# Gaps between SBUF tiles, so that the right operand of every matrix product starts 64 bytes past its left operand modulo 256

## The chip, the core and the metric

One NeuronCore of a Trainium2 chip runs the whole kernel in one launch. The metric is device time in microseconds (us) for one execution. All other times below are from one profiled execution.

## The reference

An attention with a sigmoid in place of the softmax, followed by a channel mix with token shift. Everything is float32 (three weight matrices arrive as float64).

```python
scores = q @ k.T / sqrt(64) - log(448)          # batch 8, 12 heads, 448 tokens, head size 64
x = (sigmoid(scores) @ v) -> (8, 448, 768)
x_prev = x shifted by one token
xk = mu_k * x + (1 - mu_k) * x_prev
xr = mu_r * x + (1 - mu_r) * x_prev
r = sigmoid(xr @ w_r)                           # 768 x 768, the "receptance"
out = r * (maximum(xk @ w_k, 0)**2 @ w_v)       # 768 x 1024, then 1024 x 768
```

## The kernel before

An SBUF tile is a range of bytes that is the same in all 128 partitions. A matrix product on TensorE (PE) has a left operand, 64 or 128 columns that are loaded into the array (the profile's PEld rows), and a right operand, 448 columns that then stream through it (the PE rows). The load for the next product runs while the present one streams. A matrix with more digits than one pass keeps is split into a high part (fp32r) and the remainder, and a product is made of three: high by high, low by high, high by low.

The program has three parts, each with an order for every engine's queue that a planner (`Plan`) works out when the program is built.

- **Attention and receptance, interleaved.** For each of 48 pairs of heads, `scores` (L326) makes three chunks of 128 keys: three fp32r products for each of two heads, whose 64 rows sit in the two halves of the array, so that two matmuls run side by side. The left operands are `kh` and `kl`, the right ones `qh` and `ql`. The last 64 keys go through `score_tails` (L335; `kn` by `qn`, plain f32). ScalarE (ACT) makes the sigmoid from PSUM into `pf` and `pt`. `weigh` (L355) and `weigh_tails` (L364) multiply `vn` by `pf` and `pt` in plain f32, which takes two passes for each product. `gather` makes the shifted mix `xr`. From pair 8 on, `receptance` blocks are put between: 6 row tiles x 3 products = 18 matmuls (L396 to L398), left `wr_hi`/`wr_lo` in the tiles `slot0` to `slot2`, right `xr`. There are 48 blocks, 864 matmuls; the last eight run after the attention. VectorE (DVE) meanwhile converts the float64 weights.
- **First steps of the channel mix** (up to about 447 us) are made ready during those last eight blocks.
- **The channel mix.** `multiply` (L620) does both large products by a recursive scheme with seven block products instead of eight: 2 stages x 4 pairs of batches x 7 products, 36 matmuls each, 2016 in all. The left operands are in seven tiles: `slotb0` for the first product of a round, `slotc0` to `slotc2` for the next three, `slot0` to `slot2` for the last three. The right operands are a ring of twelve tiles `rr`, nine of them allocated in one place (`rr` in the profile) and three elsewhere (`rrb`); each has a high part and, 1792 bytes on, a low part. The results go to the PSUM banks `xb` and `yb`.

Where a tile lies follows from the order in which tiles are taken from their pools, left pools from low addresses up and right pools from high addresses down. Every offset that a product uses inside a tile (512, 1536, 1792, 2048, 3072, 3584 bytes and so on) is a multiple of 256, so a tile's start modulo 256 holds for all operands in it.

Of the kernel before, what the change touches and what calls it, by code (L numbers as in the profile page):

```python
# [8 lines left out]
F32 = mybir.dt.float32  # L9
F32R = mybir.dt.float32r  # L10
# [88 lines left out]
def attention_then_channel_mix(  # L99
# [15 lines left out]
    P = 128  # L115
    N, _, S = q.shape
# [36 lines left out]
    WP, PFB, PTB, LEAD, RAW = 512, 9, 2, 2, 4  # L153
# [5 lines left out]
    def ring(pool, name, bufs, shape, dtype):  # L159
        return [pool.tile(shape, dtype, name=f"{name}{i}") for i in range(bufs)]  # L160

    wp = ctx.enter_context(tc.tile_pool(name="wp", bufs=1, side="left"))
    rp, cv, att = ExitStack(), ExitStack(), ExitStack()
    rpool = rp.enter_context(tc.tile_pool(name="rpool", bufs=1, side="left"))
    cpool = cv.enter_context(tc.tile_pool(name="cpool", bufs=1, side="left"))
    ka = ctx.enter_context(tc.tile_pool(name="ka", bufs=1, side="right"))
    slots = ring(ka, "slotb", 1, [P, 2 * WO], F32R)
    wop = ring(ka, "wop", 1, [P, WO], F32)
    apool = att.enter_context(tc.tile_pool(name="apool", bufs=1, side="right"))
    ps, psc = ExitStack(), ExitStack()  # L170
    psum = ps.enter_context(tc.tile_pool(name="psum", bufs=1, space=PSUM))
# [2 lines left out]
    wr_slots = ring(wp, "slot", 3, [P, 2 * WO], F32R)  # L174
    wr_at = [wr_slots[t // 4][:, t % 4 * DM:(t % 4 + 1) * DM] for t in range(2 * NJ)]
    wr_hi, wr_lo = wr_at[0::2], wr_at[1::2]
    xr = ring(rpool, "xr", NJ, [P, 2, 2 * S], F32R)
    ro = ring(rpool, "ro", 2, [P, S], F32)
    wraw = ring(cpool, "wraw", 2, [P, WP, 2], U32)
    wbits = ring(cpool, "wbits", 8, [P, WP], U32)  # L180
    wexpo = ring(cpool, "wexpo", 1, [P, WP], U32)
    qn = ring(apool, "qn", RAW, [P, S], F32)
    kn = ring(apool, "kn", RAW, [P, S], F32)
    vn = ring(apool, "vn", 5, [P, NV, D], F32)
    qh = ring(apool, "qh", LEAD, [P, S], F32R)
    ql = ring(apool, "ql", LEAD, [P, S], F32R)
    kh = ring(apool, "kh", LEAD, [P, KW], F32R)
    kl = ring(apool, "kl", LEAD, [P, KW], F32R)
    pf = ring(apool, "pf", PFB, [P, 2, S], F32)
    pt = ring(apool, "pt", PTB, [P, 2, S], F32)  # L190
    xx = ring(apool, "xx", 2, [P, S + 1], F32)
# [309 lines left out]
    RB, YB = 9, 15  # L501
    kp = ctx.enter_context(tc.tile_pool(name="kp", bufs=1, side="right"))
    slots += ring(kp, "slotc", 3, [P, 2 * WO], F32R) + wr_slots
    wop += ring(kp, "wopb", 1, [P, WO], F32)
    x2 = ring(kp, "x2", 2, [P, S + 1], F32)
    ys = ring(kp, "ys", YB, [P, S], F32)
    rr = ring(kp, "rr", RB, [P, 2, S], F32R)
    for x in x2:
        nc.gpsimd.memset(x[:, 0:1], 0.0)

# [81 lines left out]
    xb = ring(pb, "xb", 4, [P, 512], F32)  # L592
    yb = ring(pb, "yb", 4, [P, 512], F32)
    vp = ctx.enter_context(tc.tile_pool(name="vp", bufs=1, side="left"))
    p1s = ring(vp, "p1s", 4, [P, S], F32)
    u2 = ring(vp, "u2", 4, [P, S], F32)
    cc = ring(vp, "cc", 5, [P, S], F32)
    rt_ = ring(vp, "rt", 3, [P, S], F32)
    ys += ring(vp, "ysb", 5, [P, S], F32)
    rr += ring(vp, "rrb", 3, [P, 2, S], F32R)  # L600
    nr[0] = nr[0] % len(rr)
    ncc, nrt = [0], [0]

# [125 lines left out]
```

## Time and profile before

| | us |
|---|---|
| median of 3 runs (861.77 to 862.41) | 862.13 |
| the profiled execution | 862.21 |
| its span, first to last instruction | 860.4 |
| PE busy | 843.5 |
| PE weight loads busy | 667.4 |
| DVE busy | 601.1 |
| ACT busy | 447.4 |

A matmul's duration in the profile reaches beyond the start of the next one, because matmuls are pipelined. So what a matmul costs is the time from its start to the start of the next; durations still tell groups apart.

### The profile page before, as it was taken

The page shows a single profiled execution, that of the slowest core. Times are in us where ns is not written, and L with a number is a line of the kernel's source. Part 1 is how long each engine was busy: PE and PEld are TensorE (multiplying, and loading weights), DVE is VectorE, ACT ScalarE, POOL GpSimd, SP SyncE. Part 2 cuts the span into 40 slices and gives each one's busy share as a digit, 9 for nine tenths or more (in the row PEclk, how much of TensorE's full clock was granted, in tenths as well). Part 3 has the DMA queues.
Part 4 walks back from the last instruction along what each step waited for, and adds up shares of the span by engine and source line. Part 5 has one row for each costly group of instructions (what it writes and reads, how often), then busy time and mean ns, then how long its engine had stood idle before and what let it go on. Part 6 is the DMA issues. An engine that isn't in the chain of part 4 may idle for free.

```text
span 860.4 us, 13233 instructions
## 1 busy us (share of the span) xinstructions
PE 843.5 (98%) x4704; PEld 667.4 (78%) x4704; DVE 601.1 (70%) x1115; ACT 447.4 (52%) x758; POOL 0.5 (0%) x8
## 2 busy tenths in 40 slices
PE   7999999999999999999999999999999999999998
PEld 3456666676666766667788999999999999999997
DVE  5999898988334323342479987969789795886955
ACT  7995555645546555464368384563746333233330
POOL 0000000000000000000000000000000000000000
PEclk9999999999999999999999999999999999999999
DMA  7878898888334433341487563343654667474415
GB/s 252 259 243 290 287 304 282 286 275 280 112 113 157 146 114 115 108 139 43 153 277 242 168 182 98 139 134 123 215 179 146 201 182 236 132 232 124 144 54 161
DMA packets 90930, 157.65 MB, mean 183 GB/s; under 512 B 10352, under 2 KB 79472, under 8 KB 90864
## 3 DMA queue, kind: packets, MB, share of 16 engines
q1 hardware_dynamic: 90864, 156.81, 55.8%
q8 instruction: 37, 0.61, 0.3%
q14 instruction: 29, 0.24, 0.1%
HBM read 98.05 MB, written 58.72 MB: 182 GB/s over the span
## 4 chain that ended last, share of the span: by engine, by line
PE 94%; ACT 3%; issue 1%; DMA 1%; DVE 1%; SPq 0%
PE xb L620 27%; PE yb L620 20%; PE av L355 12%; PE sc L326 10%; PE sc L396 7%; PE sc L398 7%; PE sc L397 7%; PE av L364 2%; PE sc L335 2%; ACT pf L347 1%; ACT t L379 1%; DMA qn<-in_q 1%; ACT qh L298 0%; ACT xx L374 0%; ACT pt L347 0%
## 5 line engine op out<-in xcount | busy, mean ns | idle before, releaser
L545 ACT CAST rr<-ys 128x448 fp32r<-128x448 f32 x135 | 73.7, 566 | 107.7 <-PE yb L620 41.7
L347 ACT ACTIVATE pf<-sc 128x896 f32<-128x896 f32 x144 | 125.4, 926 | 5.2 <-PE sc L326 5.2
L355 PE MATMUL av<-pf,vn 128*64 128x448 f32 x576 | 114.4, 544 | 0.0
L396 PE MATMUL sc<-xr,slot 128*128 128x448 f32 x288 | 107.8, 374 | 2.1 <-ACT pf L347 2.1
L398 PE MATMUL sc<-xr,slot 128*128 128x448 f32 x288 | 105.7, 367 | 0.0
L397 PE MATMUL sc<-xr,slot 128*128 128x448 f32 x288 | 105.6, 367 | 0.0
L620 PE MATMUL yb<-rr,slot 128*128 128x448 f32 x450 | 93.9, 364 | 0.0
L620 PE MATMUL xb<-rr,slotc 128*128 128x448 f32 x450 | 93.1, 362 | 0.8 <-ACT p1s L649 0.8
L546 DVE TENSOR_TENSOR rr<-ys,rr 128x448 fp32r<-128x448 f32 x135 | 80.4, 617 | 15.9 <-ACT rr L545 15.7
L299 DVE TENSOR_TENSOR kl<-kn,kh 128x384 fp32r<-128x384 f32 x48 | 26.7, 556 | 92.6 <-ACT kh L298 90.9
L620 PEld LDWEIGHTS xb<-rr,slotc 128*128 128x128 f32 x450 | 84.3, 188 | 6.9 <-ACT p1s L649 1.2
L620 PEld LDWEIGHTS yb<-rr,slot 128*128 128x128 f32 x450 | 84.4, 188 | 6.7
L355 PEld LDWEIGHTS av<-pf,vn 128*64 128x64 f32 x576 | 38.9, 136 | 62.5 <-issue 61.0
L402 ACT ACTIVATE ro<-sc 128x448 f32<-128x448 f32 x48 | 26.1, 544 | 79.3 <-PE sc L398 60.8
L326 PE MATMUL sc<-qh,kh 64*128 64x448 f32 x288 | 59.5, 409 | 7.4 <-ACT qh L298 4.4
L396 PEld LDWEIGHTS sc<-xr,slot 128*128 128x128 f32 x288 | 54.0, 188 | 13.7 <-ACT pf L347 8.4
L347 ACT ACTIVATE pt<-sc 128x896 f32<-128x896 f32 x24 | 22.2, 923 | 75.9 <-PE sc L335 75.9
L398 PEld LDWEIGHTS sc<-xr,slot 128*128 128x128 f32 x288 | 54.1, 188 | 5.0
L376 DVE COPY xx<-av 128x448 f32<-128x448 f32 x38 | 22.0, 621 | 51.4 <-PE av L364 51.4
L397 PEld LDWEIGHTS sc<-xr,slot 128*128 128x128 f32 x288 | 54.1, 188 | 4.7
L326 PEld LDWEIGHTS sc<-qh,kh 64*128 64x128 f32 x288 | 27.3, 186 | 37.7 <-issue 19.3
L326 PE MATMUL sc<-ql,kh 64*128 64x448 f32 x288 | 53.5, 368 | 0.0
(86 smaller groups left out, 1377.5 us busy)
## 6 DMA issues: line engine op xcount, KB each, us to landing
k_d<-cc SPq DMA_DIRECT2D x64, 224.0 KB, 2.0
kn<-in_k SPq DMA_DIRECT2D x48, 224.0 KB, 4.4
qn<-in_q SPq DMA_DIRECT2D x48, 224.0 KB, 4.7
vn<-in_v SPq DMA_DIRECT2D x48, 224.0 KB, 3.2
x_d<-xx SPq DMA_DIRECT2D x48, 224.0 KB, 3.8
r_d<-ro SPq DMA_DIRECT2D x48, 224.0 KB, 2.7
x<-x_d SPq DMA_DIRECT2D x48, 224.0 KB, 2.6
rt<-r_d SPq DMA_DIRECT2D x48, 224.0 KB, 2.9
```

The source lines that it names most:

```text
L299: op(DVE, dve(w), at, lambda src=src, hi=hi, lo=lo: nc.vector.tensor_sub(lo[i], src, hi[i]), R + [(a + "h", i)], [(a + "l", i)])
L326: nc.tensor.matmul(sc[u][:, h, :S], kk[half[h], c * P:(c + 1) * P], qq[half[h], :], start=e == 0, stop=e == 2)
L347: op(ACT, act(2 * S), at, lambda: nc.scalar.activation(f, sc[u][:, :, :S], AF.Sigmoid, bias=NEG_LOG_S, scale=SCALE), R, [K])
L355: nc.tensor.matmul(av[n % 2][half[h], :S], vn[n % 5][:, h * NC + c, :], pf[i][:, h, :], start=c == 0, stop=False)
L376: op(DVE, dve(S), at, lambda: nc.vector.tensor_copy(x[:, 1:], av[n % 2][:, :S]), [("av", n % 2)], [X])
L396: nc.tensor.matmul(t[:, :S], wr_hi[j][:, rows], hi, start=(j == 0), stop=False)
L397: nc.tensor.matmul(t[:, :S], wr_lo[j][:, rows], hi, start=False, stop=False)
L398: nc.tensor.matmul(t[:, :S], wr_hi[j][:, rows], lo, start=False, stop=(j == NJ - 1))
L402: op(ACT, act(S), at, lambda: nc.scalar.activation(ro[u], t[:, :S], AF.Sigmoid), [tk], [("ro", u)])
L545: op(ACT, act(S, True), at, lambda: nc.scalar.copy(r[:, 0], y), [Y], [R])
L546: op(DVE, dve(S), at, lambda: nc.vector.tensor_sub(r[:, 1], y, r[:, 0]), [Y, R], [R + ("lo",)])
L620: nc.tensor.matmul(bank[:, :S], a, b, start=first and t == 0 and e == 0, stop=t == n - 1 and e == 2, skip_group_check=True)
```

## The change

`gap` takes a tile that nobody uses, and by that shifts the tiles allocated after it. `qn`, `rr` and `ys` also change places with others. The built programs have the same instructions in the same order on every engine, with the same waits on the same semaphore values; the addresses alone differ. These are the starts modulo 256 in the two programs, and how far the right operand lies past the left one:

```
products           left tile  right tile   before: left right  past    after: left right past
scores             kh, kl     qh, ql              160   160      0            160   224   64
score tails        kn         qn                  160   160      0            160   224   64
weigh              vn         pf                  160   160      0            160   224   64
weigh tails        vn         pt                  160   160      0            160   224   64
receptance         slot       xr                   32    32      0             32    96   64
channel mix        slotc      rr                  160   224     64             32    96   64
channel mix        slotb      rrb                 224    32     64             32    96   64
channel mix        slotc      rrb                 160    32    128             32    96   64
channel mix        slot       rr                   32   224    192             32    96   64
channel mix        slotb      rr                  224   224      0             32    96   64
channel mix        slot       rrb                  32    32      0             32    96   64
```

```diff
+    def gap(pool, name, size):
+        pool.tile([P, size // 4], F32, name=name)
+
...
     wop = ring(ka, "wop", 1, [P, WO], F32)
+    gap(ka, "gap4", 192)
...
+    gap(rpool, "gap0", 64)
     xr = ring(rpool, "xr", NJ, [P, 2, 2 * S], F32R)
...
-    qn = ring(apool, "qn", RAW, [P, S], F32)
     kn = ring(apool, "kn", RAW, [P, S], F32)
     vn = ring(apool, "vn", 5, [P, NV, D], F32)
+    gap(apool, "gap1", 64)
+    qn = ring(apool, "qn", RAW, [P, S], F32)
     qh = ring(apool, "qh", LEAD, [P, S], F32R)
     ql = ring(apool, "ql", LEAD, [P, S], F32R)
+    gap(apool, "gap2", 192)
     kh = ring(apool, "kh", LEAD, [P, KW], F32R)
     kl = ring(apool, "kl", LEAD, [P, KW], F32R)
+    gap(apool, "gap3", 64)
     pf = ring(apool, "pf", PFB, [P, 2, S], F32)
...
     slots += ring(kp, "slotc", 3, [P, 2 * WO], F32R) + wr_slots
+    gap(kp, "gap5", 64)
+    rr = ring(kp, "rr", RB, [P, 2, S], F32R)
+    ys = ring(kp, "ys", YB, [P, S], F32)
     wop += ring(kp, "wopb", 1, [P, WO], F32)
     x2 = ring(kp, "x2", 2, [P, S + 1], F32)
-    ys = ring(kp, "ys", YB, [P, S], F32)
-    rr = ring(kp, "rr", RB, [P, 2, S], F32R)
+    gap(kp, "gap6", 128)
...
+    gap(vp, "gap7", 64)
+    rr += ring(vp, "rrb", 3, [P, 2, S], F32R)
     p1s = ring(vp, "p1s", 4, [P, S], F32)
...
     ys += ring(vp, "ysb", 5, [P, S], F32)
-    rr += ring(vp, "rrb", 3, [P, 2, S], F32R)
```

## Rows read from the trace of the kernel before

**Rows 1.** Windows: busy us of each engine by stage, granted clock, DMA share and rate.
```profile
core 0: us, PE busy (x) PEld busy (x) DVE busy (x) ACT busy (x) POOL busy (x), PEclk, DMA share, GB/s
0.00:80.00 80.00, 69.45 (x463) 37.41 (x464) 66.14 (x141) 66.48 (x112) 0.33 (x6) 1.00 0.78 252
...
120.00:140.00 20.00, 20.00 (x124) 14.04 (x123) 19.25 (x39) 10.36 (x16) 0.00 (x0) 1.00 0.94 317
...
215.00:430.00 215.00, 215.00 (x1312) 145.06 (x1309) 77.07 (x142) 109.01 (x171) 0.13 (x2) 1.00 0.36 120
...
456.00:857.00 401.00, 400.27 (x1980) 371.21 (x1980) 321.87 (x567) 180.54 (x332) 0.00 (x0) 1.00 0.52 164
```

**Rows 2.** Waits of PE from 80 us on: us in total, times, longest.
```profile
PE xb L620 <- issue: 1.4, 1, 1.4
PE xb L620 <- ACT p1s L649: 0.8, 1, 0.8
```

**Rows 3.** Instructions by line, PE, channel mix: busy us, mean ns, idle before.
```profile
L620 PE MATMUL xb<-rr,slotc 128*128 128x448 f32 x450 | 93.1, 362 | 0.8 <-ACT p1s L649 0.8
L620 PE MATMUL xb<-rrb,slotb 128*128 128x448 f32 x63 | 13.3, 363 | 0.0
L620 PE MATMUL yb<-rr,slot 128*128 128x448 f32 x450 | 93.9, 364 | 0.0
L620 PE MATMUL xb<-rr,slotb 128*128 128x448 f32 x225 | 47.1, 365 | 1.4 <-issue 1.4
L620 PE MATMUL xb<-rrb,slotc 128*128 128x448 f32 x126 | 26.9, 365 | 0.0
L620 PE MATMUL yb<-rrb,slot 128*128 128x448 f32 x126 | 27.3, 368 | 0.0
```

**Rows 4.** Chain that ended last, channel mix: start us, us, what.
```profile
463.31 7.20 PE yb L620 x36
470.51 7.34 PE xb L620 x36
...
485.13 7.28 PE xb L620 x36
...
528.52 7.43 PE yb L620 x36
```

**Rows 5.** Matmuls that read rrb or slotc: duration ns min/median/max, first and last start.
```profile
L620 PE MATMUL yb<-rr,slotc x198: 360/363/368, 463.2 to 824.9; 128*128 128x448 f32 x198
```

**Rows 6.** Receptance, by line: busy us, mean ns, idle before.
```profile
L396 PE MATMUL sc<-xr,slot 128*128 128x448 f32 x288 | 107.8, 374 | 2.1 <-ACT pf L347 2.1
L397 PE MATMUL sc<-xr,slot 128*128 128x448 f32 x288 | 105.6, 367 | 0.0
```

**Rows 7.** Timeline of PE inside one pair's scores, two matmuls side by side.
```profile
339.20 0.37 PE L326 MATMUL sc<-qh,kl 64*128 64x448 f32 x2
...
340.64 0.37 PE L326 MATMUL sc<-ql,kh 64*128 64x448 f32 x2
```

**Rows 8.** Attention's matmuls by line: duration ns min/median/max, first and last start.
```profile
L326 PE MATMUL sc<-qh,kh x288: 358/365/738, 4.4 to 402.7; 64*128 64x448 f32 x144
L355 PE MATMUL av<-pf,vn x576: 539/539/591, 13.3 to 415.2; 128*64 128x448 f32 x192
L335 PE MATMUL sc<-qn,kn x192: 536/536/587, 9.2 to 400.9; 64*64 64x448 f32 x192
L364 PE MATMUL av<-pt,vn x192: 536/562/587, 20.1 to 416.2; 64*64 64x448 f32 x192
```

**Rows 9.** Chain that ended last, end of receptance and first channel-mix product.
```profile
446.08 1.42 issue
447.49 3.90 PE xb L620 x18
```

**Rows 10.** DVE's remainders of rr and rrb from 456 us on: busy us, mean ns, idle.
```profile
L546 DVE TENSOR_TENSOR rr<-ys,rr 128x448 fp32r<-128x448 f32 x127 | 75.4, 617 | 15.7 <-ACT rr L545 15.7
...
L546 DVE TENSOR_TENSOR rrb<-ys,rrb 128x448 fp32r<-128x448 f32 x39 | 23.3, 618 | 2.4 <-ACT rrb L545 2.4
```

## The prediction

> **What bounds the kernel now.** I read the windows by stage first. Before 80 us PE is busy for 69.45 of 80 us and waits for the engines around it. [...] The list of PE's waits confirms it: after 80 us there are two, of 1.4 and 0.8 us [rows 2], both where receptance hands over to the channel mix. So a nanosecond that a matmul loses or gains after 80 us is a nanosecond of the kernel, as long as no other engine is about to become the bound. The one place where another nearly is, is around 130 us: DVE is busy for 19.25 of 20 us and the DMA engines for 0.94 of the time. In the channel mix DVE has 321.87 of 401 us, ACT half of that [rows 1].
>
> Then I ask whether a matmul's cost depends on where its operands lie. The channel mix answers that by itself, because one source line with one shape runs there on six pairings of tiles. The chain gives the cost of 36 matmuls, the rows by line give the mean duration of one for each pairing:
>
> - slotc by rr, 64 bytes past: 7.20 us for 36, that is 200.0 ns each; mean duration 362.
> - slot by rr, 192 past: 7.28 us, 202.2 ns; mean 364.
> - slotc by rrb, 128 past: 7.34 us, 203.9 ns; mean 365.
> - slot by rrb, 0 past: 7.43 us, 206.4 ns; mean 368 [rows 3, 4].
>
> Duration less 162 ns is the cost, to within 0.5 ns, in all four; so the two pairings that have no piece of their own in the chain can be read too: slotb by rr, 0 past, mean 365, 203 ns; slotb by rrb, 64 past, mean 363, 201 ns [rows 3]. The reader is to see that this is no property of a tile: slotc is the quick one with rr and not with rrb, slotb is the quick one with rrb and not with rr. What goes with the cost is the distance of the two operands. Both pairings at 64 are the cheapest, both at 0 are dearer.
>
> **The change, part by part.** No instruction, order or wait differs, so nothing is added or moved; the reserved bytes cost no time. The sum is over the products whose distance becomes 64, each priced by its present cost less the 200 ns (duration 362) of the pairing that has 64 now.
>
> *Channel mix, 2016 matmuls.* 711 are at 64 already (450 + 198 of slotc by rr, 63 of slotb by rrb): nothing. Slot by rr: 450 + 198 = 648 times (364 - 362) = 1.3 us. Slotb by rr: 225 x 3 = 0.7 us. Slotc by rrb: 126 + 90 = 216 x 3 = 0.65 us. Slot by rrb: 216 x 6 = 1.3 us. Together 3.9 us. (Of each pair of counts one row stands in the list; the other row, with x198 or x90, has the same mean within 1 ns.)
>
> *Receptance, 864 matmuls, all at 0.* The second and third lines have means of 367 (the first, 374, holds the stalls with which blocks begin) [rows 6]. If they come to 362: 864 x 5 = 4.3 us. This is not quite a copy of the channel mix: there the high and the low right operand alternate 1792 bytes apart, here three products in a row read addresses that agree modulo 512. That order at 64 is not in the trace. Bounds: nothing from below, and 367 - 360 = 7 ns from above, the shortest single duration that slotc by rr shows [rows 5], 6.0 us. I take 5 ns, because the two pairings at 64 agree within 1 ns although their high and low parts stand the other way round modulo 512.
>
> *Scores, 432 double matmuls, at 0.* Eight starts in a row span 1.44 us, 205.7 ns from one to the next [rows 7], and the median duration is 365 with a minimum of 358 [rows 8]. Two matmuls in the two halves of the array at distance 64 are in no row. Bounds: nothing, and the 7 ns to the minimum. I take 4 ns, toward the nearest rows (205.7 to about 201), and count 330 of the 432: those before 80 us are hidden in PE's waits, and one in nine ends in a change to another kind of product, whose pause the address has no part in. 1.3 us, at most 2.3.
>
> *Plain f32 products* (weigh and both kinds of tails), at 0. Weigh is 539 in the minimum and in the median, the key tails 536 in both [rows 8]: no scatter, while the scores, also at distance 0, have 358 and 365. I cost them at nothing. The cover for that is that an f32 pass streams more slowly: 448 columns in about 377 ns (539 less the same 162), nearly twice the 200 of an fp32r product, so a weight read has more room beside it. If that cover fails it is the slower rival below.
>
> *Other engines.* Addresses move for DVE, ACT and DMAs as well. DVE's remainders for rr (start 224 modulo 256) take 617 ns and for rrb (start 32) 618 [rows 10]: nothing.
>
> *What is not kept.* Two receptance blocks run before 80 us beside PE's waits (36 x 5 = 0.2 us). The last eight blocks (144 x 5 = 0.7 us) end in a wait of 1.42 us before the first channel-mix product [rows 9]; the chain names nothing that ended it ("issue"), but that product's operands come from loads through ACT and DVE, which an earlier PE would find no earlier. I lose half of the 0.7. Together 0.55 us.
>
> Sum: 3.9 + 4.3 + 1.3 - 0.55 = 9.0 us. The profiled execution took 862.21, 0.08 over the median of the runs, and 1.8 over its span; so 862.2 - 9.0 = 853.2 us.
>
> [...] The rows show 362 to 368 ns, 200.0 to 206.4 ns start to start, for the same product under different distances [rows 3, 4]. [...]
>
> **Rivals.**
>
> 1. *Only the channel mix gains* (5 in 100). Its distances are priced by rows of its own; receptance and scores might not be helped, if in their order of operands 64 is as bad as 0. Against it: slotb by rrb and slotc by rr are two orders, and both are quick. 862.2 - 3.9 = 858.3 us.
>
> 2. *Another engine becomes the bound between 80 and 215 us* (5 in 100). There DVE converts weights with the DMA engines at 0.94 near 130 us [rows 1], and about 135/366 of what runs between 80 and 446 us lies in that stretch, by time 305 of 828 receptance matmuls and 120 of 330 double ones: 305 x 5 + 120 x 4 = 2.0 us would turn into waits. Against: PE has no wait at all in it now, and its queue would come only 2% sooner to DVE's work. 853.2 + 2.0 = 855.2 us.
>
> [...]
>
> 4. *Slower: the f32 passes leave their flat level* (4 in 100). Weigh and tails make 288 + 48 + 48 = 384 passes (576 rows in pairs, 192 in fours). They were never seen at 64. If each went from 539 to the 591 that is their longest now [rows 8], 384 x 52 = 20 us, and the sum is 862.2 - 9.0 + 20 = 873 us. It decides from 9.0 / 384 = 23 ns a pass on, and makes the kernel slower by over 0.2% from 28 ns on. For it: an f32 pass loads 64 columns beside a stream of another pace, so its best distance need not be that of fp32r. Against: f32 at distance 0 shows no loss at all, and a slower stream has room.
>
> **The numbers.** The forecast has 80 in 100, with the time of its sum, 853.2 us. The range: with the upper bounds of receptance and scores 862.2 - 3.9 - 6.0 - 2.3 = 850.0; with the lower bounds 858.3, which takes in rivals 1 and 2. Outside are rivals 3 and 4 and a few in 100 of misjudged sizes. A measurement of this kernel tells 0.2%, 1.7 us, from no change. Faster by more: forecast and rivals 1 and 2, 90 in 100; within: 6; slower: 4.
>
> **What would show it.** In the profile after, all six pairings of L620 have a mean of 362 to 363, and every 36 matmuls in the chain take 7.20 to 7.25 us where no stall is; receptance's second and third lines have 362, the scores' median is near 360, weigh stays at 539. The first channel-mix product starts some 5 us earlier than at 447.49 us [rows 9], and the channel mix is about 4 us shorter. The prediction is wrong if receptance stays at 367, if weigh rises above 539, if PE's list of waits between 80 and 440 us is no longer empty, or if pairings at 64 still differ from each other.

## The result and the profile after

The changed kernel takes 852.93 us (median of 6 runs, 852.26 to 854.2), the kernel before 861.95 (6 runs, 859.24 to 863.33): a ratio of 0.9903, 95% interval 0.9887 to 0.9919, so 9.0 us faster. The two profiled executions differ by 862.21 - 852.26 = 9.95 us.

The matmuls of the changed kernel by line and shape (count, busy us, mean ns of one, idle before); line numbers have moved, L633 is `multiply`, L406 to L408 are receptance, L365 is weigh:

```profile
L365 PE MATMUL av<-pf,vn 128*64 128x448 f32 x576 | 114.4, 544 | 0.0
L406 PE MATMUL sc<-xr,slot 128*128 128x448 f32 x288 | 106.6, 370 | 2.1 <-ACT pf L357 2.1
L407 PE MATMUL sc<-xr,slot 128*128 128x448 f32 x288 | 104.3, 362 | 0.0
...
L633 PE MATMUL xb<-rr,slotc 128*128 128x448 f32 x450 | 93.0, 362 | 0.4 <-ACT p1s L662 0.4
L633 PE MATMUL yb<-rr,slot 128*128 128x448 f32 x450 | 92.9, 362 | 0.0
...
L633 PE MATMUL xb<-rr,slotb 128*128 128x448 f32 x225 | 46.5, 362 | 1.4 <-issue 1.4
...
L633 PE MATMUL xb<-rrb,slotc 128*128 128x448 f32 x126 | 26.5, 362 | 0.0
L633 PE MATMUL yb<-rrb,slot 128*128 128x448 f32 x126 | 26.5, 362 | 0.0
...
L633 PE MATMUL xb<-rrb,slotb 128*128 128x448 f32 x63 | 13.2, 362 | 0.0
```

The reader is to see that the six pairings, 362 to 368 before [rows 3], are one number now, and that receptance's second and third lines came down by 5 ns, from 367 to 362, its first one by 4 [rows 6]. The chain that ended last (start us, us, what) agrees: 7.20 us for every 36 matmuls, where there were 7.20, 7.28, 7.34 and 7.43 [rows 4].

```profile
457.49 7.20 PE yb L633 x36
464.69 7.20 PE xb L633 x36
471.89 7.20 PE yb L633 x36
479.09 7.20 PE xb L633 x36
```

PE's waits after 80 us (us in total, times, longest) have not grown; the second one has halved [rows 2]:

```profile
PE xb L633 <- issue: 1.4, 1, 1.4
PE xb L633 <- ACT p1s L662: 0.4, 1, 0.4
```

And by stage (busy us by engine, clock, DMA share and rate) PE is as full as before, beside a DVE that is no more of a bound than it was [rows 1]:

```profile
120.00:140.00 20.00, 20.00 (x126) 13.91 (x126) 18.63 (x37) 10.58 (x17) 0.00 (x0) 1.00 0.95 325
...
450.00:846.00 396.00, 395.98 (x1980) 371.09 (x1980) 320.97 (x565) 180.91 (x332) 0.00 (x0) 1.00 0.52 166
```

Where the time came from, by the starts of matmuls in the two traces: the first channel-mix product starts at 442.14 us instead of 447.49 (5.35 us), and from there to the start of the last matmul it is 403.79 us instead of 408.41 (4.62 us). Together 9.97, which is the whole difference of the two spans (860.4 and 850.5 us).

The attention's durations (ns min/median/max, first and last start): the scores came down by 2 ns in the first row's median and by 3 in the second, whose row before stands on top; weigh did not move [rows 8].

```profile
L326 PE MATMUL sc<-qh,kl x288: 355/362/572, 4.9 to 402.9; 64*128 64x448 f32 x144
...
L336 PE MATMUL sc<-qh,kh x288: 357/363/739, 4.5 to 397.9; 64*128 64x448 f32 x144
L336 PE MATMUL sc<-qh,kl x288: 357/359/572, 5.0 to 398.1; 64*128 64x448 f32 x144
...
L365 PE MATMUL av<-pf,vn x576: 539/539/590, 12.9 to 410.2; 128*64 128x448 f32 x192
```

### The profile page after: what moved, and what is told of

It is laid out like the page before. It is cut to its first block, busy times and chain, and to the rows that moved or that the text cites. A ratio compares the mean times of both kernels' runs of the same rounds, so it can differ in the third digit from the quotient of the medians.

```text
span 850.5 us, 13233 instructions
## 1 busy us (share of the span) xinstructions
PE 834.7 (98%) x4704; PEld 667.2 (78%) x4704; DVE 600.5 (71%) x1115; ACT 447.6 (53%) x758; POOL 0.5 (0%) x8
## 4 chain that ended last, share of the span: by engine, by line
PE 90%; ACT 4%; DMA 3%; issue 1%; DVE 1%; SPq 0%; POOLq 0%; POOL 0%; DVEq 0%; ACTq 0%
PE xb L633 26%; PE yb L633 20%; PE av L365 12%; PE sc L336 10%; PE sc L406 6%; PE sc L407 6%; PE sc L408 6%; DMA x<-x_d 2%; PE av L374 2%; PE sc L345 2%; ACT pf L357 1%; ACT t L389 1%; DMA qn<-in_q 1%; ACT qh L308 0%; ACT xx L384 0%
## 5 line engine op out<-in xcount | busy, mean ns | idle before, releaser
L365 PE MATMUL av<-pf,vn 128*64 128x448 f32 x576 | 114.4, 544 | 0.0
L406 PE MATMUL sc<-xr,slot 128*128 128x448 f32 x288 | 106.6, 370 | 2.1 <-ACT pf L357 2.1
L407 PE MATMUL sc<-xr,slot 128*128 128x448 f32 x288 | 104.3, 362 | 0.0
L408 PE MATMUL sc<-xr,slot 128*128 128x448 f32 x288 | 104.2, 362 | 0.0
L633 PE MATMUL xb<-rr,slotc 128*128 128x448 f32 x450 | 93.0, 362 | 0.4 <-ACT p1s L662 0.4
L633 PE MATMUL yb<-rr,slot 128*128 128x448 f32 x450 | 92.9, 362 | 0.0
L633 PEld LDWEIGHTS xb<-rr,slotc 128*128 128x128 f32 x450 | 84.3, 187 | 6.4 <-ACT p1s L662 0.8
L633 PEld LDWEIGHTS yb<-rr,slot 128*128 128x128 f32 x450 | 84.4, 187 | 5.6
L365 PEld LDWEIGHTS av<-pf,vn 128*64 128x64 f32 x576 | 38.9, 136 | 62.4 <-issue 61.3
L406 PEld LDWEIGHTS sc<-xr,slot 128*128 128x128 f32 x288 | 54.0, 188 | 12.6 <-ACT pf L357 8.3
L408 PEld LDWEIGHTS sc<-xr,slot 128*128 128x128 f32 x288 | 54.0, 187 | 3.7
```

The costliest lines, as they stand in the source:

```text
L365: nc.tensor.matmul(av[n % 2][half[h], :S], vn[n % 5][:, h * NC + c, :], pf[i][:, h, :], start=c == 0, stop=False)
L406: nc.tensor.matmul(t[:, :S], wr_hi[j][:, rows], hi, start=(j == 0), stop=False)
L407: nc.tensor.matmul(t[:, :S], wr_lo[j][:, rows], hi, start=False, stop=False)
L408: nc.tensor.matmul(t[:, :S], wr_hi[j][:, rows], lo, start=False, stop=(j == NJ - 1))
L633: nc.tensor.matmul(bank[:, :S], a, b, start=first and t == 0 and e == 0, stop=t == n - 1 and e == 2, skip_group_check=True)
```

## The experiments

The theory: what a fp32r matmul costs beyond the 200.0 ns of the cheapest pairing [rows 4] depends on the distance of its right operand to the left operands, modulo 256. Rivals: the new order of the tiles made the gain, or the place of one operand alone. In the `all_at` runs one number, DIST, replaces 64 in the changed kernel's gaps; the order of the tiles, the instructions and their order stand as in the changed kernel. `gap` now takes its size modulo 256, and `gap6` makes up for `gap5`. The attention's tiles as a whole lie 64 - DIST bytes further on modulo 256 than in the changed kernel.

```diff
-        pool.tile([P, size // 4], F32, name=name)
+        if size % 256:
+            pool.tile([P, size % 256 // 4], F32, name=name)
...
-    gap(rpool, "gap0", 64)
+    gap(rpool, "gap0", DIST)
...
-    gap(apool, "gap1", 64)
+    gap(apool, "gap1", DIST)
...
-    gap(apool, "gap2", 192)
+    gap(apool, "gap2", 256 - DIST)
...
-    gap(apool, "gap3", 64)
+    gap(apool, "gap3", DIST)
...
-    gap(kp, "gap5", 64)
+    gap(kp, "gap5", DIST)
...
-    gap(kp, "gap6", 128)
+    gap(kp, "gap6", 192 - DIST + 256)
...
-    gap(vp, "gap7", 64)
+    gap(vp, "gap7", DIST)
```

**All distances 0** (DIST = 0).

> The changed kernel with every right operand back at distance 0 modulo 256 from its left one, in the changed kernel's order of tiles (rr before ys, kn before qn and so on). Distance theory: the gain goes again. Channel mix: mean durations back to about 365 (as slotb by rr, whose parts stood in this order modulo 512, 203 ns each), receptance's second and third lines back to 367, scores' median to 364 or 365, weigh 539. 2016 x 2.8 + 864 x 5 + 330 x 4 = 11.3 us more than 852.9: about 864 us. Rival, the other order of the tiles made the gain (other neighbours for what DVE and ACT write): the time stays at 853, with 362 for the channel mix.

Measured: 861.23 us, median of 10 runs, ratio to the kernel before 1.0021 (0.9992 to 1.005), where about 864 was expected. Mean durations of 365 in the channel mix and in receptance:

```profile
L410 PE MATMUL sc<-xr,slot 128*128 128x448 f32 x288 | 105.2, 365 | 0.0
L636 PE MATMUL xb<-rr,slotc 128*128 128x448 f32 x450 | 94.2, 365 | 0.5 <-ACT p1s L665 0.5
```

So the gain hangs on the distance, not on the order of the tiles, which is the changed kernel's here. Two things were off. Receptance has the very addresses that it had before, and costs 365 instead of 367. And two of the ten runs took 867.99 and 870.84 us, the other eight 859.74 to 862.18.

**Both operands 64 bytes on** (distance 64 kept).

```diff
-    gap(ka, "gap4", 192)
+    gap(ka, "gap4", 384)
...
+    gap(wp, "gap8", 64)
     wr_slots = ring(wp, "slot", 3, [P, 2 * WO], F32R)
```

> Distance 64 kept, but both operands of every product 64 bytes further on: left at 96 and right at 160 modulo 256 in receptance and channel mix, left 224 and right 32 in the attention. Distance theory: nothing changes, 852.9 us, 362 for receptance and channel mix. Rival, the place of one operand alone counts (left at 32 or right at 96): the groups go back toward 364 to 368 and the time toward 858 to 864.

Measured: 853.65 us, median of 4 runs, ratio 0.9915 (0.99 to 0.993).

```profile
L408 PE MATMUL sc<-xr,slot 128*128 128x448 f32 x288 | 104.4, 363 | 0.0
...
L634 PE MATMUL yb<-rr,slot 128*128 128x448 f32 x450 | 92.9, 362 | 0.0
L634 PE MATMUL xb<-rr,slotc 128*128 128x448 f32 x450 | 92.9, 362 | 0.0
```

Both operands have moved by 64 bytes and the matmuls cost what they did, so the place of one operand alone does not explain the gain.

**The other distances.** DIST = 128, then 32, 96 and 192, then 160 and 224.

> Every distance 128. Distance theory: all pairings of the channel mix like slotc by rrb before, mean 365 with singles from 358 to 373; receptance and scores 2 to 4 ns dearer than at 64; 852.9 + 2016 x 3.5 + 864 x 3.5 + 330 x 3 = 864 us. Rival, only distance 0 is bad and all else is good: 853. Weigh 539 in both.

> Every distance 32. In the runs so far the start-to-start times within one run of like products settle into a repeating pattern: 200.0 ns on average at 64, 204.0 at 128, 202.2 at 192, and at 0 either 202.7 or 206.7. If the collision is between pieces of 64 bytes, 32 lies half in the piece of 0 and half in that of 64 and comes out between, 200 to 203: 853 to 860 us. If any gap that keeps the two streams apart will do, 200.0 and 853 us. Rival, 32 is worse than 0: over 861.

> Every distance 96, half way from 64 to 128. Pieces of 64 bytes: between 200.0 and 204.0 ns, 853 to 863 us. If 64 is only the edge of a good stretch: 200.0 or less and 853 us or less; under 852 us it would beat the changed kernel.

> Every distance 192. By the channel mix before (slot by rr, 364, 202.2 ns): all L620-like groups at 364, receptance at 364 too, scores between; 852.9 + 2016 x 2.2 + 864 x 2.2 + 330 x 2 = 860 us. Rival, the price of 192 came from the mixture of pairings then: 362 and 853.

> Every distance 160, between 128 (204.0 ns) and 192 (202.2). As 32 and 96 lay above both their neighbours or near the dearer one (206.6 and 205.3), 160 should too: 203 to 206 ns, mean 365 to 368, 861 to 868 us. If it falls to 200.0 (362) or under, a second good distance exists.

> Every distance 224, which is 32 bytes before the left operand. Same thought: 203 to 207 ns, mean 365 to 369, 861 to 871 us; if 362 or less, a second good distance.

Measured: 862.74 us at 128; 871.01 at 32 (4 runs, ratio 1.0114, 1.0086 to 1.0141); 868.73 at 96 (4 runs, ratio 1.0101, 1.0073 to 1.0129); 861.58 at 192; 853.06 at 160; 862.62 at 224 (one run each where none is given). One row of the channel mix from each, in the order 32, 96, 128, 160, 192, 224:

```profile
L636 PE MATMUL yb<-rr,slot 128*128 128x448 f32 x450 | 95.9, 369 | 0.0
```

```profile
L636 PE MATMUL yb<-rr,slot 128*128 128x448 f32 x450 | 95.3, 367 | 0.0
```

```profile
L636 PE MATMUL yb<-rr,slot 128*128 128x448 f32 x450 | 94.7, 366 | 0.0
```

```profile
L636 PE MATMUL yb<-rr,slot 128*128 128x448 f32 x450 | 92.9, 362 | 0.0
```

```profile
L636 PE MATMUL yb<-rr,slot 128*128 128x448 f32 x450 | 93.9, 364 | 0.0
```

```profile
L636 PE MATMUL yb<-rr,slot 128*128 128x448 f32 x450 | 94.4, 365 | 0.0
```

In 36 matmuls' worth of the chain at 160 the cost is the changed kernel's 7.20 us:

```profile
458.33 7.20 PE yb L636 x36
465.53 7.20 PE xb L636 x36
```

In the channel mix and in receptance only 64 and 160 are at 362. That 160 is as good as 64 there was not expected: the thought that 32 and 96 would lie between their neighbours failed at 32 (206.6 ns by the starts, as dear as 0 at its dearest) and at 96 (205.3, dearer than 64 and 128), and 160 is cheaper than both of its own. So the price does not go by pieces of 64 bytes that collide or don't. Why 64 and 160 are the cheap ones, no run shows. Single starts in the trace show one more difference: at 64 the times from start to start go round 202, 201, 197, at 160 nearly every one is 200. The mean is the same. At 192 receptance's second and third lines, expected at 364 each, have 367 and 361, by the starts 202.2 ns on average as in the channel mix.

For the scores, whose matmuls run two side by side, 160 is not good. From 80 us on, the starts of their double matmuls inside a chain lie 205.2 ns apart on average, against 201.2 at 64 and 204.6 in the kernel before. The row at 160, to be set beside 357/359/572 at 64:

```profile
L339 PE MATMUL sc<-qh,kl x288: 359/364/572, 5.1 to 398.7; 64*128 64x448 f32 x144
```

At 32 the 206.6 ns are not the only price either. Receptance's last eight blocks and the first channel-mix product ran at 200.0 ns in the same execution. Receptance's second line from 418 to 447 us, then from 333 to 340 us:

```profile
L410 PE MATMUL sc<-xr,slot 128*128 128x448 f32 x48 | 17.4, 362 | 0.0
```

```profile
L410 PE MATMUL sc<-xr,slot 128*128 128x448 f32 x12 | 4.4, 369 | 0.0
```

Weigh, in plain f32, has a mean of 544 ns at all eight distances. The median of the score tails is 536 and that of weigh's tails 562, also at all eight. The mean of the score tails moves between 537 and 554, because single early ones last up to 1007 ns.

**A low part alone at 0.** The third tile of `slot` is moved on by 64 bytes, and the high parts of receptance's weights are kept in the tiles before it.

```diff
-    wr_slots = ring(wp, "slot", 3, [P, 2 * WO], F32R)
+    wr_slots = ring(wp, "slot", 2, [P, 2 * WO], F32R)
+    gap(wp, "gap0", 64)
+    wr_slots += ring(wp, "slotd", 1, [P, 2 * WO], F32R)
...
-    wr_hi, wr_lo = wr_at[0::2], wr_at[1::2]
-    gap(rpool, "gap0", 64)
+    wr_hi, wr_lo = wr_at[:NJ], wr_at[NJ:]
...
-    gap(vp, "gap7", 64)
```

> Only slot's third tile lies 64 bytes further on, so that its left operands are at distance 0; it holds the low parts of four of the six row tiles of receptance (the high parts and the other low ones stay at 64), and one of the seven products of the channel mix. In receptance the second matmul of three uses a low part, and that part is loaded while the first one streams. Theory A, what counts is the distance of a streaming operand to the weights loaded beside it for the next matmul: the first line of receptance pays, by 4/6 x 5 = 3 ns start to start, and the second one nothing. Theory B, what counts is the distance to the matmul's own weights: the second line pays 3 ns, the first nothing. Either way the one channel-mix product at 0 (288 matmuls) goes from 362 to about 365 and the others stay; total about 852.9 + 0.9 + 0.8 = 854.6 us.

Measured: 854.5 us, one run.

```profile
L407 PE MATMUL sc<-xr,slot 128*128 128x448 f32 x288 | 107.0, 371 | 2.1 <-ACT pf L358 2.1
L409 PE MATMUL sc<-xr,slot 128*128 128x448 f32 x288 | 104.3, 362 | 0.0
...
L408 PE MATMUL sc<-xr,slotd 128*128 128x448 f32 x192 | 69.8, 364 | 0.0
...
L633 PE MATMUL yb<-rr,slotd 128*128 128x448 f32 x225 | 48.0, 368 | 0.0
...
L633 PE MATMUL yb<-rr,slot 128*128 128x448 f32 x225 | 46.5, 362 | 0.0
```

The channel mix does its part: the one product at 0 (slotd) costs 368 beside 362 for its neighbours in the same run. Receptance pays less, and not in one line: 371 for 370 in the first and 364 for 362 in the second. By the starts its matmuls take 200.8 ns on average for 200.1 in the changed kernel, so three together pay 2.2 ns, 0.6 to 1.0 in each line. In four of the six row tiles one matmul in three is at 0; at the prices of unbroken rows at 0 (202.7 or 206.7 less 200) the three would pay 1.8 or 4.5 ns. Theory A wanted all of it in the first line, theory B all of it in the second, so this run doesn't tell them apart; that stays open.

**Distance 0 with the attention moved, and again.** Addresses as in `all_at_0`, with the attention's tiles 64 bytes lower, left and right alike.

```diff
     t1 = ring(apool, "t1", 2, [P, S], F32)
+    gap(apool, "gap9", 64)
```

> All distances 0 as in all_at_0, and the addresses of receptance and channel mix too; only the attention's tiles lie 64 bytes lower, left and right alike (160 modulo 256, as in the kernel before; 224 in all_at_0). In the kernel before most receptance blocks ran at 206.7 ns a matmul, in all_at_0 nearly all at 202.7, with the same addresses of their own. Theory, distance 0 has two steady states and the matmuls just before a block pick the one: receptance goes back to a mean of 367 (205 to 206 ns) and the time to about 862 to 864 us, with the channel mix still at 365. Rival, the state is a matter of the execution or the chip: receptance stays at 365.

> The very kernel of zero_moved_attention once more, in several executions. There the channel mix ran at 206.7 ns a matmul, while all_at_0, with the same addresses in the channel mix, ran at 202.7. If an execution picks between two steady states by chance, the executions fall on two levels some 2016 x 4.0 = 8 us apart, near 860 and 868 us, as two of ten of all_at_0 already did (867.99 and 870.84 beside 859.74 to 862.18). If the attention's addresses pick the state, all lie near 868 us.

Measured: 867.75 us in the one run of the first; 863.8 us in the second (10 runs, ratio 1.0034, 0.9995 to 1.0073). Both profiles show the channel mix at 206.7 ns a matmul from its second product on (the first is at 202.8), not at the 202.7 that its addresses had given in `all_at_0`. Chain of `all_at_0`, then of `zero_again`:

```profile
460.81 7.29 PE yb L636 x36
468.10 7.30 PE xb L636 x36
```

```profile
461.80 7.44 PE yb L637 x36
469.24 7.44 PE xb L637 x36
```

Receptance, expected at 367, had 366 in the first profile and 367 in the second, which is the same program. The theory that the attention's addresses pick the state fell on the channel mix, which was to stay at 365 and went to 368. What the runs do show is that at distance 0 the same addresses give 7.30 us in one program and 7.44 in another, and that one program's executions spread, nine of the ten of `zero_again` from 859.62 to 872.27 us (the tenth took 872.87), while the kernel before spread from 858.81 to 863.2 beside it. They are not two clean levels: 862.72 and 864.88 lie between.

The trace of `zero_again` shows that one execution can mix them: each unbroken stretch of matmuls there runs at one of two paces, and holds it to its end. Of receptance's 21 stretches 8 ran at 202.7 ns and 13 at 206.5 to 206.7. The third line from 386 to 393 us, then from 418 to 446 us:

```profile
L412 PE MATMUL sc<-xr,slot 128*128 128x448 f32 x10 | 3.6, 365 | 0.0
```

```profile
L412 PE MATMUL sc<-xr,slot 128*128 128x448 f32 x45 | 16.6, 368 | 0.0
```

The kernel before does the same in receptance, 5 stretches of 21 at 202.5 to 202.7 and 16 at 206.5 to 206.7. The channel mix, from its second product on, is one stretch of 1980 matmuls, so its pace alone is worth 8 us, and the mixture in receptance some 3 us more (both estimates, from 4.0 ns a matmul). That would give two groups of times with a spread in each, as 859.62 to 864.88 and 869.5 to 872.87, but only the profiled executions have a trace. What picks the pace stays open.

**Fewer columns.**

```diff
-                    nc.tensor.matmul(bank[:, :S], a, b, start=first and t == 0 and e == 0, stop=t == n - 1 and e == 2, skip_group_check=True)
+                    w_ = S if t == 0 and e == 0 else S - 32
+                    nc.tensor.matmul(bank[:, :w_], a, b[:, :w_], start=first and t == 0 and e == 0, stop=t == n - 1 and e == 2, skip_group_check=True)
```

> The changed kernel, distance 64, with 32 of the 448 columns left out of the channel mix's products except the first of each block (so its outputs are not the reference's). It asks what the 200.0 ns are that are left. If the streaming of columns sets them, a matmul of 416 columns takes 32 x 200/448 = 14 ns less, and 36 matmuls with 32 or 33 narrow ones 6.75 us: 56 x 0.45 = 25 us less, about 828 us. If the loading of the 128 left columns sets them, 36 matmuls still take 7.20 us and the time stays at 853.

Measured: 833.42 us, one run, 19.5 us less than the changed kernel where the streaming theory wanted 25.

```profile
458.24 6.83 PE yb L634 x36
465.07 6.84 PE xb L634 x36
```

With the 4 full matmuls of 36 at 200 ns, the 32 narrow ones take (6.84 - 0.80) / 32 = 189 ns, 11 less for 32 columns fewer, where the streaming theory wanted 14 and the loading theory nothing. The single starts agree: 188.5 ns on average after a narrow matmul (mostly 190, 191, 182 and 183), 203.8 after a full one. So at distance 64 most of the cost goes with the length of the stream, and the loading of the left columns alone does not set it. Why some 3 of the 14 ns are missing stays open.

## Why the prediction was right

**PE bounds all of it after 80 us**: right. PE's waits after 80 us did not grow, and what its matmuls lost the kernel lost. One reading is looser than it says: duration less 162 ns gives 203 for slotc by rrb, and its piece of the chain gave 203.9. Over all its starts that pairing took 203.4, so the prices hold.

**The cost goes with the distance**: shown for fp32r products, by 0 taking the gain away in the new order of tiles, by 64 giving it at other addresses, and by the scan. It was read from six pairings that the kernel before happened to have; the crossing of slotb and slotc over rr and rrb was the evidence, and it held.

**Channel mix, 3.9 us**: measured 4.62 from the first to the last start; of it about 0.4 us is the shorter wait before the second product, so 4.2 for the matmuls.

**Receptance and scores, 4.3 + 1.3 - 0.55 = 5.05 us** up to the first channel-mix product: measured 5.35. The receptance lines fell from 367 to 362 as forecast, though its order of operands modulo 512 had no row; by the starts that is 3.9 us from the third block on. The scores' 4 ns were too much: 2 to 3 ns in the medians, and 0.8 us where 1.3 was forecast. The loss of 0.55 did not come. The third receptance block, the first after PE's early waits, starts at 78.86 us instead of 79.47, which is the remaining 0.6 us. And the wait at the hand-over stayed 1.4 us, since the loads there came forward with PE: the first load of `x` is issued at 416.2 us instead of 421.2. So two errors of about half a microsecond stood against each other, and that the sum came out to 0.3 us is partly luck. The chain that ended last has changed there: between 416 and 446 us it ran through receptance before, now it runs through these loads. The longest of them (start us, us, what):

```profile
420.47 7.18 DMA x<-x_d
```

PE waits there for only 0.4 us, before the second product. What a still quicker receptance would gain was not tried.

**Plain f32 unchanged**: right, 544 ns for weigh at all eight distances. The stated cover, a slower stream with more room for a weight read, was not tested by itself. In the trace before, weigh's pairs of passes start 376 ns apart and its loads take 136 ns, where receptance's matmuls start 205 ns apart and its loads take 188:

```profile
L397 PEld LDWEIGHTS sc<-xr,slot 128*128 128x128 f32 x288 | 54.1, 188 | 4.7
...
L355 PEld LDWEIGHTS av<-pf,vn 128*64 128x64 f32 x576 | 38.9, 136 | 62.5 <-issue 61.0 <-DVE wbits L227 0.3 <-DMA vn<-in_v 0.3
```

**A price for each distance**: this is the step that was right in the sum and too simple in itself. At 0 there is no one price: 202.7 ns in one stretch and 206.7 in another. Receptance's 205 and slot by rrb's 206.4, read as prices of an order of operands, were such states, or mixtures of them. The sum is sound because it used what that execution had paid, and because 64 showed only one level: every unbroken stretch of receptance, and the long one of the channel mix, in the changed kernel and in `both_64_on` is at 200.0 to 200.2 ns. That the one profiled execution, 862.21 us, lay so near the median of all runs, 861.95, was luck: the kernel before has scattered from 858.81 to 863.54.

**The rivals.** No effect of the distance, the 6 in 100 for an unchanged time: excluded for fp32r, whose durations go from 362 to 369 ns by distance alone and whose kernel gained 9.0 us; for plain f32 no run contradicts it (weigh's mean is 544 ns at every distance). Whether it is the loads that slow the stream, no run shows by itself. Channel mix alone, another bound at 80 to 215 us, f32 leaving its level: none happened.

## What to carry to other kernels

Where TensorE is the bound and products are fp32r, compare the matmul durations of one line and shape by the tiles that they read; if they differ, work out the tiles' starts modulo 256 and group by the distance of right and left. Here the channel mix's six pairings had 362 to 368 ns at four distances and 362 at one. 64 bytes were good for every kind of fp32r product and worth 1% over a mixture of distances (852.93 us against 861.95). 160 was as good in one run (853.06 us), but not for the products that run two side by side (205.2 ns against 201.2). 32 and 96 were worse in the median (871.01 and 868.73 us) than distance 0 (861.23 and 863.8). Take the distance from runs, since the eight that were tried follow no obvious rule; only steps of 32 were tried, and only right operands of 448 columns but for one run with 416. A kernel whose times scatter from execution to execution may be at a distance with more than one steady state, as here at 0 (202.7 and 206.7 ns a matmul, 859.62 to 872.87 us); then one profile does not give the price.

## What the runs showed of the hardware that was not expected

At equal addresses and equal instructions, runs of fp32r matmuls fall into repeating patterns that last as long as the run of matmuls does: 36 in 7.20 us at distances 64 and 160, 7.30 or 7.44 at distance 0, and at 32 either 200.0 or 206.7 ns a matmul. Distance 64 takes away most of the scatter as well: 852.26 to 854.2 us in 6 runs at 64, against 859.62 to 872.27 in nine of `zero_again`. And what is left at 64 goes with the columns: 200 ns for 448, 189 for 416.
